# A scan block and two feed-forward layers on one core: one decay transfer per block, and three GpSimd products moved to other engines

## The chip, the cores and the metric

The kernel runs on one core of a Trainium2 chip. The time is the device time of one execution in microseconds (us), and it is given as the median of a few runs. The five engines of the core are called PE (TensorE, matrix products), DVE (VectorE), ACT (ScalarE), POOL (GpSimd) and SP (SyncE, which here only issues transfers). Each works through its own instructions in their order.

## The reference, cut to what matters

```python
# a state-space scan over 4 batches x 8 heads, 768 positions, D = 32, N = 16
log_a = np.log(np.clip(a, 1e-06, 1.0))
for c in range(nc):                              # chunks; state is carried over
    cum = np.cumsum(la, axis=-1)
    L = np.exp(cum[:, :, :, None] - cum[:, :, None, :]) * causal
    M = np.einsum('bhin,bhjn->bhij', Cc, Bc) * L
    y_intra = np.einsum('bhij,bhjd->bhid', M, xc)
    y_inter = np.einsum('bhin,bhnd->bhid', Cc, state) * np.exp(cum)[:, :, :, None]
    y[:, :, sl] = y_intra + y_inter
    Bx = np.einsum('bhjn,bhjd->bhjnd', Bc, xc) * np.exp(cum[:, :, -1:] - cum)[..., None, None]
    state = np.exp(np.sum(la, axis=-1))[:, :, None, None] * state + np.sum(Bx, axis=2)
# then two layers on the 3072 x 256 result, d_ff = 2048
h = x @ w_in;  g = softplus(h);              x = g @ w_out
h = x @ w2_in; g = a smoothed relu of h;     x = g @ w2_out
```

## The kernel before

**Tiling.** The kernel cuts the 768 positions into six blocks `c` of 128 and treats the four batches `b` apart, so that there are 24 units `u = 4c + b` of the scan. A unit holds 8 heads. For each unit the kernel loads x, B and C (`load`, tile `u`) and the rows of the decays (`rows`, tile `ld`), turns the latter into the 128x1024 matrix of decays by a scan on DVE (`decay`, line 745; in block 0 by two products on PE and an Exp on ACT, lines 738 and 747), multiplies the scores C B (`scores`, PE, line 781, one job for two units) by it in two halves (`weigh`, line 790, DVE), and multiplies the result with x on PE (`out`, lines 814 to 826). `evac` (ACT, line 839) and `ready` (DVE, lines 848 and 850) carry the 256 values per position out of PSUM as a high and a low part, `xh` and `xl`.

**Carried state.** From block 1 on three small products join them, all on POOL. `sources` (line 753) weighs B by the last column of the decays, `cd` (line 765) weighs C by the running decays in tile `dec`, and `sm` (line 858) makes two masked copies of the state. `dec` is loaded once per block `c` from a DRAM scratch, by eight transfers, one per head (line 728). In block 0, `sources` is done in two halves, on POOL too.

**Feed-forward steps.** Each layer is 96 or more steps `s`: `up` (PE, lines 881 to 883, three products for each pair of high and low parts), an activation `g` (ACT line 905 in layer one, ACT and DVE in layer two), its split into `g_hi` and `g_lo` (line 920, DVE or POOL), and `down` (PE, line 946). In the first eight steps `down` uses the unsplit weight instead (`whole`, line 934). The weights come in 64-bit form, 16 pieces `j` of 128x512 per layer, into four staging buffers `st` (`load_w`, line 539). Five or six instructions take each piece apart: `w0` and `w1` (ACT or DVE, lines 555, 551, 563, 569), `w2` (DVE, line 575 or 580), `w3` (DVE, line 587), `w_hi` (line 492 or 494) and `split_w` (line 597, DVE or POOL). A staging buffer is free after `w3`.

**Order.** `program()` writes the order of all of it as the kernel is built. It adds each job with its engine or engines, an assumed cost, what it needs, which buffers it takes and returns, and a due time; `Jobs.order` then takes the jobs one by one by a list schedule on assumed times. Where a job has a choice of engines, the constant `BIAS` is added to POOL's time before the two are compared. The constants from `WHOLE` to `WARM` (lines 382 to 412) feed this planner, and so a change in one of them can reorder every engine. What the planner assumes is not what the chip does, and the engines keep the written order whatever happens.

**Fillers.** Before line 1027 the loop puts idle products on PE (line 1022) where the planned gap before a PE job is long, in the first 26 us of the plan only.

Of the kernel before, what the change touches and what calls it, by code (L numbers as in the profile page):

```python
# [7 lines left out]
F32 = mybir.dt.float32  # L8
# [18 lines left out]
class Jobs:  # L27
# [4 lines left out]

    LATENCY = {PE: 200, ACT: 230, DVE: 220, POOL: 200, SP: 1900}

    def __init__(self):
        self.jobs = {}
# [7 lines left out]
    def order(self, slots, begin):  # L46
# [51 lines left out]
        for _ in range(len(jobs)):  # L98
            best = []
            for name in ready:  # L100
                options, _, _, takes, _, _ = jobs[name]
                got = pick(takes, min(at[name].values()))
                if got is None:
                    continue
                starts = {e: max(got[0], at[name][e], clock[e]) for e in options}
                bias = lambda e: BIAS_2 if e == POOL and name[0] == "split_w" and name[1] else BIAS.get(e, 0)
                _, start, engine = min((starts[e] + cost + bias(e), starts[e], e) for e, cost in options.items())
                best.append((start, due[name], number[name], name, engine, got[1]))
            assert best, [(name, jobs[name][3]) for name in ready]
            first = min(best)  # L110
            start, _, _, name, engine, got = min(
                (b for b in best if b[4] == first[4] and b[0] <= first[0] + (PATIENCE if first[0] > EARLY else HASTE)), key=lambda b: (b[1], b[0], b[2])
            )
            options, _, _, _, gives, size = jobs[name]
            for tag, i in got:
                free[tag] = [f for f in free[tag] if f[1] != i]
            held[name] = got
            result.append((name, engine, got))
            cost = options[engine] * (1.9 if engine == PE and start < COLD else 1.0)
            if engine in (DVE, POOL):  # L120

                kind = name if isinstance(name, str) else name[0]
                other = POOL if engine == DVE else DVE
                for a, b, k in busy[other][-3:]:
                    shared = max(0.0, min(b, start + cost) - max(a, start))
                    cost += shared * SHARED[engine].get(kind, 0.0) * (k > 0)
                    if b == clock[other]:
                        clock[other] += shared * k * (SHARED[engine].get(kind, 0.0) > 0)
                busy[engine].append((start, start + cost, SHARED[engine].get(kind, 0.0)))
            clock[engine] = start + cost  # L130
            end = clock[engine]
            if engine == SP:
                pipe = max(pipe, end) + size / RATE
                end = pipe
            done = self.done[name] = end
            end += self.LATENCY[engine]
            self.start[name], self.end[name] = start, end
            if name == ("ready", NU - 1):
                free["z"] += [(end, 0), (end, 1)]
            for other in gives:  # L140
                kept = held[other[1]] if other[0] == "part" else held.pop(other)
                for tag, i in [kept[other[2]]] if other[0] == "part" else kept:
                    free[tag].append((end, i))
            ready.remove(name)
            for other in after[name]:
                for e in at[other]:

                    at[other][e] = max(at[other][e], done + 80 if e == engine != SP else end)
                missing[other] -= 1
                if missing[other] == 0:  # L150
                    ready.add(other)
# [38 lines left out]
def program():  # L190
# [33 lines left out]
    add("clip", DVE, 350, needs=["clip_load", "sums"])  # L224
    add("store", SP, 800, needs=["clip"], size=98e3)
    add("runs", DVE, 1500, needs=["clip", ("columns", 1)])
    add("store_runs", SP, 400, needs=["runs"], size=98e3, gives=["clip_load"])
    for c in range(1, NC):
        add(("dec", c), SP, 400 * DEC_DMAS, needs=["store_runs"], takes=["dec"], size=262e3)
    for u in range(NU):  # L230
# [12 lines left out]
        else:  # L243
            add(("rows", u), SP, 400, needs=["store"], takes=["ld"], size=524e3)
            add(("decay", u), DVE, 2220, needs=[("rows", u)])
            decay = [("decay", u)]
            add(("cd", u), POOL, 400, needs=[("load", u), ("dec", c)])
        if c == 0:
            for hg in range(2):
                add(  # L250
                    ("sources", u, hg), POOL, 400, takes=["bt"] * (hg == 0),
                    needs=[("load", u), ("decay", u, hg)] + ([("sources", u, 0)] if hg else []),
                )
        elif c < NC - 1:
            add(("sources", u), POOL, 450, needs=[("load", u)] + decay, takes=["bt"])
        if b % 2:
            v = u // 2
            add(
# [23 lines left out]
        if c > 1:  # L282
            needs += [("split_w", 0, kind, j) for kind in "io" for j in range(8) if place_of(kind, j) == c]
            needs += [("down", s) for s in range(WHOLE)]
        due = when(first_step[c, b] - LEAD if c < 2 else min(first_step[c, b] - LEAD, CHUNK * (c - 1) + SPACE * b + SHIFT))
        add(("evac", u), ACT, 270 + 150 * (c == 0), needs=needs)
        add(
# [1 line left out]
            gives=[("out", u)] + [("dec", c)] * (b == NB - 1 and c > 0),  # L289
        )  # L290
        if c < NC - 1:
            add(("sm", u), POOL, 330, needs=[("ready", u)])


    last_use, first_use = {}, {}
# [5 lines left out]
    for m in range(2):  # L301
        for j in sorted(range(8), key=lambda j: first_use[m, j]):
            for kind in "io":
                w = (m, kind, j)
                add(("load_w", *w), SP, 400, takes=["st"], size=524e3)
                add(
                    ("w0", *w), {ACT: 580} if signed(*w) else {ACT: 580, DVE: 350}, needs=[("load_w", *w)] + [("ready", NU - 1)] * m, takes=["w32"] * m,
                )
# [13 lines left out]
    for s, (m, c, t0, n, fc, m_fc) in enumerate(steps):  # L322
# [38 lines left out]
        if fc + m_fc == NFC:  # L361
            root = ("down", min(r for r in range(len(steps)) if steps[r][:3] == (m, c, t0)))
            for e in range(2):
# [7 lines left out]
                    )  # L371
                else:
                    add(("store", s, e), SP, 400, due=own, needs=[("finish_hi", s, e)], gives=[("finish_hi", s, e)], size=262e3)
    slots = dict(h=2, y=1, z=0, acc=4, t=2, g=N_G, gh=3, gl=3, ld=5, u=4, bc=3, bt=3, dec=2, st=4, w32=16, osb=4)
    result = jobs.order(slots, {POOL: 3700, ACT: 2000, PE: 4000, DVE: 800})
    return jobs, steps, result


# [2 lines left out]
]  # L381
WHOLE = 8
ACT_UNTIL = 120
H_MORE = 8
H_ALL = 84
GL_POOL = 84
COLD = 0.0
KEEP = 26000.0
FILL = 0.8
SHARED = {  # L390
    DVE: {"w1": 1.1, "w2": 0.95, "w3": 0.95, "decay": 0.36, "split_w": 0.3, "g_lo": 0.1, "clip": 0.3, "runs": 0.3},
    POOL: {"g_lo": 0.25, "weigh": 0.4, "sources": 1.0, "cd": 1.1, "sm": 0.6, "split_w": 0.4},
}
WEIGH_POOL = []
PRELU = (0, 0)
LOW_ACT = 1
BIAS = {DVE: 0, POOL: 500}
PATIENCE = 0
EARLY = 30000.0
HASTE = 0  # L400
CHUNK = 16
BIAS_2 = 2000
RATE = 250.0
BEGIN = 14000.0
STRETCH = 1.0
LEAD = 1
SPACE = 4
SHIFT = 2
LAG = 3000
DEC_DMAS = 8  # L410
N_G = 3
WARM = 10

# [2 lines left out]


@with_exitstack
def tile_kernel(ctx: ExitStack, tc: tile.TileContext, al, bc, ub, w_in, w_out, w2_in, w2_out, out):

# [53 lines left out]
    for tag, dtype, n in (("xh", F32R, NC), ("xl", F32R, NC), ("ld", F32, 5), ("gh", F32R, 3), ("gl", F32R, 3), ("u", F32, 4), ("dec", F32, 2)):  # L476
        for i in range(n):
            new(f"{tag}{i}", dtype, tag) if tag in ("xh", "xl", "gh", "gl") else buf(tag, i)
    raw_t = [base.tile([128, 2, 256, 2], U32, name=f"st{i}") for i in range(4)]
    eye_t = base.tile([128, H * Q], F32, name="eye_t")  # L480
    sm_t = [base.tile([128, 64], F32, name=f"sm{b}") for b in range(NB)]
# [1 line left out]
    idle, eye16, later = (base.tile([128, Q], BF16, name=n) for n in ("idle", "eye16", "later"))  # L483

    xh, xl, xw = {}, {}, {}
    clip_z = dram.tile([NU * 2, 4, Q], F32, name="clip_z")
    clip_p = dram.tile([NU * 2, 4, Q], F32, name="clip_p")
    engines = {ACT: nc.scalar, DVE: nc.vector, POOL: nc.gpsimd}

    def copy(engine, out, in_):  # L490
# [23 lines left out]
    spare += [("ld", 4, 0), ("ld", 4, 1), ("bc", 2, 0), ("w32", 0, 0)] + [("u", i, 0) for i in range(4)]  # L514

    def raw(*w):
        t = raw_t[got["load_w", *w][0][1]]
        return t[:, :, :, 0], t[:, :, :, 1], t

    def w32(m, kind, j):  # L520
# [98 lines left out]
    def a_load(engine):  # L619

        first = new(of("a_load"), F32, "first")
        tiles["a"] = [first[:, i * Q:(i + 1) * Q] for i in range(3)]
        src = al[0:2 * NB].rearrange("r (h i) -> (r h) i", h=4)
        nc.sync.dma_start(tiles["a"][0], src.unsqueeze(0).to_broadcast([4, 32, Q]))
        nc.gpsimd.memset(tiles["a"][2], 1.0)

    @job
# [54 lines left out]
    def store(engine, *step):  # L682
# [3 lines left out]
            for i in range(0, T, n):  # L686
                nc.sync.dma_start(out[steps[s][1], e, :, i:i + n], osb(s, e)[:, i:i + n])
        else:
            nc.sync.dma_start(clip_z, z_t)

    @job
    def runs(engine):
# [5 lines left out]

    @job
    def store_runs(engine):  # L700
        nc.sync.dma_start(clip_p, tiles["clip"])

    @job
    def load_bc(engine, v):
# [12 lines left out]
    @job  # L717
    def rows(engine, u):

        rows_of = clip_z.rearrange("(u g) h i -> u (g h i)", g=2)  # L720
        nc.sync.dma_start(flat(ld_t(u)), rows_of[u:u + 1].to_broadcast([128, H * Q]))

    @job
    def dec(engine, c):
        t = mine("dec", c)[0]
        src = clip_p.rearrange("(c b g) h i -> c (g h) b i", b=NB, g=2)[c]
        for h in range(H):
            nc.sync.dma_start(t[h * N:(h + 1) * N], src[h:h + 1].to_broadcast([N, NB, Q]))

    def ld_t(u):  # L730
        return buf(*got["rows", u][0]) if u >= NB else buf(*got["spread", u, 0][1])
# [18 lines left out]
    def sources(engine, u, hg=None):  # L750

        h = slice(0, H) if hg is None else slice(4 * hg, 4 * hg + 4)
        nc.gpsimd.tensor_tensor(
            out=bt_t(u)[:, h], in0=parts(u)[1].rearrange("p (h n) -> p h n", n=N)[:, h],
            in1=ld_t(u)[:, h, Q - 1:Q].to_broadcast([128, h.stop - h.start, N]), op=ALU.mult,
        )
# [5 lines left out]
    def cd(engine, u):  # L762

        t = parts(u)[2]
        nc.gpsimd.tensor_tensor(out=t, in0=t, in1=mine("dec", u // NB)[0][:, u % NB, :], op=ALU.mult)

    def cb_t(u, hg):
        banks = got["scores", u // 2]
# [86 lines left out]
    @job  # L855
    def sm(engine, u):
        b = u % NB
        nc.gpsimd.tensor_tensor(
            out=sm_t[b].rearrange("p (e d) -> p e d", e=2), in0=s_t[b].rearrange("p (e d) -> p e d", e=2),
            in1=of_one.unsqueeze(2).to_broadcast([128, 2, D]), op=ALU.mult,  # L860
        )


    root = {}
# [208 lines left out]
```

## Time and profile before

| | |
|---|---|
| runs | 607.69, 606.53, 604.54 us; median 606.53 us |
| the profiled execution | 607.7 us, of which the span of instructions is 606.0 us |
| busy share of the span | PE 97%, DVE 78%, ACT 40%, POOL 11% |
| mean granted clock of PE | 0.993 |
| instructions | 9263 |

A row of the profile gives the start of an instruction in us from the span's start, its duration, the engine, the line of the kernel and the tiles as out<-in, and in brackets how long the engine sat idle before it and what ended that. PE's matrix products overlap, so a busy PE is not always a PE at its best rate; the granted clock (1.00 is 2.4 GHz, 0.50 is 1.2 GHz) is listed beside it.

### The profile page before, as it was taken

To read this page: it belongs to the slowest core of one execution; us is meant where nothing else is said; L and a number is where in the kernel's file an instruction comes from. 1 tells how busy PE (TensorE), PEld (TensorE's weight loads), DVE (VectorE), ACT (ScalarE), POOL (GpSimd) and SP (SyncE) were. 2 spreads that over 40 slices of the span, in tenths; PEclk is the share of its full clock that TensorE was granted. 3 is DMA by queue.
4 is the path that set the end of the run, shared out by engine and by line. 5 is a ranking of instruction groups with operands and counts; after the bars stand their busy time and mean duration, and the time that the engine had idled before them with its cause. 6 is when DMAs were issued, how large, how long until landed. Compare 5 with 4: busy or idle time off the path is not lost.

```text
span 606.0 us, 9263 instructions
## 1 busy us (share of the span) xinstructions
PE 587.9 (97%) x3588; PEld 484.7 (80%) x3588; DVE 471.1 (78%) x758; ACT 239.6 (40%) x415; POOL 66.9 (11%) x88
## 2 busy tenths in 40 slices
PE   7897989999999999999999999999999999999997
PEld 3685989998877777777788888888888888888886
DVE  7878999666575765535899986678899898899895
ACT  4544663322222322322576876654232231322321
POOL 4215553310211100000100000000000000000000
PEclk9898999999999999999999999999999999999999
DMA  7975543412322212000344000000000000000000
GB/s 278 322 245 192 180 157 131 131 54 96 104 80 70 79 54 70 1 0 1 105 140 140 35 1 0 2 1 36 35 2 0 36 1 1 36 0 2 35 1 35
DMA packets 22208, 43.69 MB, mean 72 GB/s; under 512 B 2308, under 2 KB 5252, under 8 KB 22164
## 3 DMA queue, kind: packets, MB, share of 16 engines
q1 hardware_dynamic: 22164, 43.10, 21.2%
q8 instruction: 28, 0.46, 0.3%
q14 instruction: 16, 0.13, 0.1%
HBM read 39.75 MB, written 3.34 MB: 71 GB/s over the span
## 4 chain that ended last, share of the span: by engine, by line
PE 88%; DVE 7%; issue 2%; ACT 1%; POOL 1%; DMA 1%; DVEq 0%; POOLq 0%; ACTq 0%
PE acc L946 41%; PE h L881 10%; PE h L882 10%; PE h L883 10%; PE acc L881 2%; PE acc L882 2%; PE acc L883 2%; DVE ld L745 2%; PE acc L934 2%; PE y L819 2%; DVE w L587 2%; PE z L883 1%; PE z L881 1%; PE z L882 1%; PE y L781 1%
## 5 line engine op out<-in xcount | busy, mean ns | idle before, releaser
L946 PE MATMUL acc<-gh,woh 128*128 128x512 f32 (+1 forms) x416 | 149.9, 368 | 0.0
L946 PE MATMUL acc<-gh,wol 128*128 128x512 f32 (+1 forms) x416 | 148.6, 365 | 0.0
L920 DVE TENSOR_TENSOR gl<-g,gh 128x512 fp32r<-128x512 f32 x178 | 125.1, 703 | 13.6 <-ACT gh L492 1.7
L881 PE MATMUL h<-xh,wih 128*128 128x512 f32 (+1 forms) x336 | 122.4, 364 | 1.4 <-ACT g L905 1.4
L882 PE MATMUL h<-xh,wil 128*128 128x512 f32 (+1 forms) x336 | 120.2, 358 | 1.9 <-DVE wil L597 1.9
L883 PE MATMUL h<-xl,wih 128*128 128x512 f32 (+1 forms) x336 | 119.7, 356 | 0.0
L946 PE MATMUL acc<-gl,woh 128*128 128x512 f32 (+1 forms) x416 | 114.1, 365 | 0.0
L494 DVE CAST gh<-g 128x512 fp32r<-128x512 f32 x128 | 54.6, 426 | 61.1 <-ACT g L905 52.8
L946 PEld LDWEIGHTS acc<-gh,woh 128*128 128x128 f32 x416 | 78.4, 188 | 14.6 <-ACT g L905 1.0
L946 PEld LDWEIGHTS acc<-gh,wol 128*128 128x128 f32 x416 | 78.5, 189 | 12.3
L946 PEld LDWEIGHTS acc<-gl,woh 128*128 128x128 f32 x416 | 73.3, 189 | 12.6
L892 ACT ACTIVATE t<-h 128x512 f32<-128x512 f32 x67 | 40.1, 599 | 108.0 <-PE h L883 103.8
L881 PEld LDWEIGHTS h<-xh,wih 128*128 128x128 f32 x336 | 63.5, 189 | 13.5 <-ACT g L905 1.8
L882 PEld LDWEIGHTS h<-xh,wil 128*128 128x128 f32 x336 | 63.6, 189 | 11.2 <-DVE wil L597 2.3
L883 PEld LDWEIGHTS h<-xl,wih 128*128 128x128 f32 x336 | 63.5, 189 | 9.1
L905 ACT ACTIVATE g<-h 128x512 f32<-128x512 f32 x51 | 30.4, 597 | 72.7 <-PE h L883 66.1
L911 DVE SCALAR_TENSOR_TENSOR t<-t 128x512 f32<-128x512 f32 x72 | 49.4, 686 | 6.5 <-ACT t L892 6.1
L745 DVE TENSOR_TENSOR_SCAN ld<-ld,eye_t 128x1024 f32<-128x1024 f32 x20 | 47.1, 2357 | 2.4 <-DMA ld<-clip_z 2.3
L912 DVE TENSOR_TENSOR g<-h,t 128x512 f32<-128x512 f32 x67 | 46.3, 692 | 2.3
L492 ACT CAST gh<-g 128x512 fp32r<-128x512 f32 x56 | 34.8, 621 | 18.7 <-DVE g L912 16.7
L905 ACT ACTIVATE g<-acc 128x512 f32<-128x512 f32 x31 | 18.5, 598 | 48.7 <-PE acc L883 48.1
L881 PE MATMUL acc<-xh,wih 128*128 128x512 f32 (+1 forms) x74 | 26.4, 356 | 0.0
(142 smaller groups left out, 668.4 us busy)
## 6 DMA issues: line engine op xcount, KB each, us to landing
ld<-clip_z SPq DMA_DIRECT2D x20, 512.0 KB, 4.0
st<-in_w_in_dram SPq DMA_DIRECT2D x16, 512.0 KB, 3.8
st<-in_w_out_dram SPq DMA_DIRECT2D x16, 512.0 KB, 4.1
u<-in_ub_dram SPq DMA_DIRECT2D x24, 256.0 KB, 3.8
bc<-in_bc_dram SPq DMA_DIRECT2D x12, 384.0 KB, 3.5
out_dram<-dec SPq DMA_DIRECT2D x6, 256.0 KB, 2.2
dec<-clip_p SPq DMA_DIRECT2D x40, 32.0 KB, 2.8
out_dram<-bc SPq DMA_DIRECT2D x5, 256.0 KB, 2.0
```

The costliest lines, as they stand in the source:

```text
L492: nc.scalar.copy(out, in_)
L494: engines[engine].tensor_copy(out, in_)
L745: nc.vector.tensor_tensor_scan(t, t, eye_t, 0.0, ALU.mult, ALU.add)
L881: nc.tensor.matmul(o, wh, xh[c][:, k, t0:t0 + n], start=(k == 0), stop=False)
L882: nc.tensor.matmul(o, wl, xh[c][:, k, t0:t0 + n], start=False, stop=False)
L883: nc.tensor.matmul(o, wh, xl[c][:, k, t0:t0 + n], start=False, stop=(k == 1))
L892: nc.scalar.activation(out=t, in_=ph, func=AF.Relu, bias=0.5, scale=0.5)
L905: nc.scalar.activation(out=g, in_=ph, func=AF.Softplus)
L911: nc.vector.scalar_tensor_tensor(out=t, in0=t, scalar=1.0, in1=t, op0=ALU.min, op1=ALU.mult)
L912: nc.vector.tensor_tensor(out=g, in0=ph, in1=t, op=ALU.max)
L920: engines[engine].tensor_tensor(out=mine("g_lo", s)[0], in0=mine("g", s)[0], in1=mine("g_hi", s)[0].bitcast(F32), op=ALU.subtract)
L946: nc.tensor.matmul(acc_t(s, e), w, g[:, j * n:(j + 1) * n], start=(begins(e, j) and g is gh and i == 0), stop=(fc + j == NFC - 1 and g is ...
```

## The change

`dec` becomes one transfer for a block instead of eight. For it the DRAM scratch `clip_p` is laid out so that a block's rows lie together, and it is written by four transfers (one for each batch) instead of one; the input `al` is ordered by batch first, and block 0's decays come as an input `a0` of their own. For blocks 1 to 5 `cd` and `sources` run on DVE and `sm` on ACT, there as two instructions; for block 0 `sources` stays on POOL. Two of block 0's `weigh` jobs (numbers 3 and 6, that is unit 1's second half and unit 3's first) go to POOL, each behind a copy of its scores by ACT. The weight pieces `j = 2` of layer one get two staging buffers `sx` in the space of block 1's `xh` and `xl`, so block 1's `evac` needs their `w3`. The planner's constants change with it.

```diff
-    LATENCY = {PE: 200, ACT: 230, DVE: 220, POOL: 200, SP: 1900}
+    LATENCY = {PE: 200, ACT: 230, DVE: 220, POOL: 200, SP: 2300}
...
+            cost += SIGNAL * (engine == DVE)
...
-    add("store_runs", SP, 400, needs=["runs"], size=98e3, gives=["clip_load"])
+    add("store_runs", SP, 1600, needs=["runs"], size=98e3, gives=["clip_load"])
...
-            add(("cd", u), POOL, 400, needs=[("load", u), ("dec", c)])
+            add(("cd", u), DVE, 200, needs=[("load", u), ("dec", c)])
...
-            add(("sources", u), POOL, 450, needs=[("load", u)] + decay, takes=["bt"])
+            add(("sources", u), DVE, 210, needs=[("load", u)] + decay, takes=["bt"])
...
+        if c == 1:
+
+            needs += [("w2" if signed(0, kind, SX) else "w3", 0, kind, SX) for kind in "io"]
...
-            add(("sm", u), POOL, 330, needs=[("ready", u)])
+            add(("sm", u), ACT, 500, needs=[("ready", u)])
...
-                add(("load_w", *w), SP, 400, takes=["st"], size=524e3)
+                add(("load_w", *w), SP, 400, takes=["sx" if m == 0 and j == SX else "st"], size=524e3)
...
-    slots = dict(h=2, y=1, z=0, acc=4, t=2, g=N_G, gh=3, gl=3, ld=5, u=4, bc=3, bt=3, dec=2, st=4, w32=16, osb=4)
-    result = jobs.order(slots, {POOL: 3700, ACT: 2000, PE: 4000, DVE: 800})
+    slots = dict(sx=2, h=2, y=1, z=0, acc=4, t=2, g=N_G, gh=3, gl=3, ld=5, u=4, bc=3, bt=3, dec=2, st=4, w32=16, osb=4)
+    result = jobs.order(slots, {POOL: 3700, ACT: 2000, PE: 5500, DVE: 2500, SP: 900})
...
-H_MORE = 8
+H_MORE = 16
-GL_POOL = 84
+GL_POOL = 16
+SIGNAL = 55.0
-WEIGH_POOL = []
+WEIGH_POOL = [3, 6]
-BIAS = {DVE: 0, POOL: 500}
+BIAS = {DVE: 0, POOL: 2000}
-BIAS_2 = 2000
-RATE = 250.0
+BIAS_2 = 9000
+RATE = 330.0
-SPACE = 4
+SPACE = 2
-LAG = 3000
-DEC_DMAS = 8
+LAG = 1500
+DEC_DMAS = 1
+SX = 2
...
-        src = al[0:2 * NB].rearrange("r (h i) -> (r h) i", h=4)
-        nc.sync.dma_start(tiles["a"][0], src.unsqueeze(0).to_broadcast([4, 32, Q]))
+        nc.sync.dma_start(tiles["a"][0], a0.unsqueeze(0).to_broadcast([4, 32, Q]))
...
-        nc.sync.dma_start(clip_p, tiles["clip"])
+        n = NC * 2
+        for b in range(NB):
+            nc.sync.dma_start(clip_p[:, :, b], tiles["clip"][b * n:(b + 1) * n])
...
-        src = clip_p.rearrange("(c b g) h i -> c (g h) b i", b=NB, g=2)[c]
-        for h in range(H):
-            nc.sync.dma_start(t[h * N:(h + 1) * N], src[h:h + 1].to_broadcast([N, NB, Q]))
+        src = clip_p.rearrange("(c g) h b i -> c (g h) (b i)", g=2)[c]
+        nc.sync.dma_start(flat(t), src.unsqueeze(1).to_broadcast([H, N, NB * Q]))
...
-        nc.gpsimd.tensor_tensor(
+        engines[engine].tensor_tensor(
             out=bt_t(u)[:, h], in0=parts(u)[1].rearrange("p (h n) -> p h n", n=N)[:, h],
...
-        nc.gpsimd.tensor_tensor(out=t, in0=t, in1=mine("dec", u // NB)[0][:, u % NB, :], op=ALU.mult)
+        nc.vector.tensor_tensor(out=t, in0=t, in1=mine("dec", u // NB)[0][:, u % NB, :], op=ALU.mult)
...
-        nc.gpsimd.tensor_tensor(
-            out=sm_t[b].rearrange("p (e d) -> p e d", e=2), in0=s_t[b].rearrange("p (e d) -> p e d", e=2),
-            in1=of_one.unsqueeze(2).to_broadcast([128, 2, D]), op=ALU.mult,
-        )
+        for e in range(2):
+            nc.scalar.activation(
+                out=sm_t[b][:, e * D:(e + 1) * D], in_=s_t[b][:, e * D:(e + 1) * D], func=AF.Copy, scale=of_one[:, e:e + 1],
+            )
```

## Rows read from the trace of the kernel before

**Rows 1.** Windows of the first 100 us: length, then each engine's busy us; at the end PE clock, DMA share, GB/s.
```profile
23.10:27.00 3.90, 3.88 (x33) 2.74 (x33) 3.47 (x7) 0.52 (x1) 0.00 (x0) 0.64 1.03 311
...
38.00:44.00 6.00, 5.09 (x43) 4.70 (x45) 6.00 (x5) 2.62 (x5) 1.11 (x2) 1.00 0.72 210
...
47.00:52.40 5.40, 5.31 (x16) 4.13 (x16) 5.40 (x8) 1.89 (x3) 2.41 (x4) 0.68 0.36 135
...
sum 100.00, PE 85.45 PEld 71.15 DVE 87.52 ACT 50.21 POOL 42.81; mean PE 4.07 PEld 3.39 DVE 4.17 ACT 2.39 POOL 2.04
```

**Rows 2.** Windows of the span: one of layer two.
```profile
320.00:340.00 20.00, 20.00 (x90) 16.57 (x89) 19.81 (x38) 12.74 (x22) 0.00 (x0) 1.00 0.38 127
```

**Rows 3.** Windows from 120 to 245 us, their sum.
```profile
sum 125.00, PE 125.00 PEld 102.39 DVE 79.41 ACT 35.53 POOL 16.73; mean PE 20.83 PEld 17.07 DVE 13.23 ACT 5.92 POOL 2.79
```

**Rows 4.** Timeline of PE to 150 us.
```profile
23.12 2.70 PE L934 MATMUL acc<-gh,w 128*128 128x256 f32 x8 [2.04 <-DVE w L587]
...
30.24 3.62 PE L934 MATMUL acc<-gh,w 128*128 128x256 f32 x16
...
40.92 0.39 PE L882 MATMUL h<-xh,wil 128*128 128x256 f32 x1 [0.91 <-DVE wil L597]
...
47.09 5.41 PE L934 MATMUL acc<-gh,w 128*128 128x256 f32 x16 [2.08 <-DVE w L587]
```

**Rows 5.** The chain that ended last, from 17 us: start, us, what.
```profile
17.25 0.76 POOL bt L753
18.01 0.26 POOL sm L858
18.27 2.46 DVE ld L790 x4
```

**Rows 6.** Groups by line and shape: busy us, mean ns | idle before, releaser.
```profile
L765 POOL TENSOR_TENSOR u<-u,dec 128x128 f32<-128x128 f32 x20 | 17.6, 886 | 20.6 <-DMA u<-in_ub_dram 20.6
L790 DVE TENSOR_TENSOR ld<-acc,ld 128x512 f32<-128x512 f32 x25 | 16.7, 680 | 0.0
...
L587 DVE SCALAR_TENSOR_TENSOR w<-st,w 128x512 uint32<-128x512 uint32 x17 | 15.0, 888 | 0.2
...
L575 DVE SCALAR_TENSOR_TENSOR w<-w,t 128x512 uint32<-128x512 uint32 x15 | 12.9, 864 | 5.0 <-ACT t L563 4.7 <-ACT w L555 0.3
...
L920 POOL TENSOR_TENSOR gl<-g,gh 128x512 fp32r<-128x512 f32 x6 | 11.5, 1921 | 61.0 <-PE acc L946 56.9 <-ACT gh L492 3.4 <-DVE gh L494 0.7
...
L597 POOL TENSOR_TENSOR wol<-w,woh 128x512 fp32r<-128x512 f32 x4 | 8.8, 2206 | 6.1 <-ACT woh L492 5.5 <-PE y L826 0.6
...
L850 DVE SCALAR_TENSOR_TENSOR s<-s,dec,y 128x64 f32<-128x64 f32 x16 | 4.3, 271 | 0.0
...
L841 ACT COPY s<-y 128x64 f32<-128x64 f32 x4 | 0.9, 218 | 0.0
```

**Rows 7.** Timeline of SP from 24 us; xN merges neighbouring issues.
```profile
24.54 10.19 SPq L728 DMA_DIRECT2D dec<-clip_p  x8
34.84 0.40 SPq L539 DMA_DIRECT2D st<-in_w_out_dram  x1
```

**Rows 8.** Waits of SP's queue over the span: us, times, longest.
```profile
SPq L539 <- DVE w L587: 33.0, 11, 7.3
...
SPq L728 <- DMA ld<-clip_z: 6.4, 6, 2.0
```

**Rows 9.** Timeline of all engines around 57 us.
```profile
55.98 2.65 POOL L597 TENSOR_TENSOR wol<-w,woh 128x512 fp32r<-128x512 f32 x1 [0.58 <-PE y L826]
...
57.47 1.71 DVE L575 SCALAR_TENSOR_TENSOR w<-w,t 128x512 uint32<-128x512 uint32 x1
...
60.44 0.68 DVE L575 SCALAR_TENSOR_TENSOR w<-w,t 128x512 uint32<-128x512 uint32 x1
```

**Rows 10.** Timeline of DVE from 47 us.
```profile
46.96 0.68 DVE L790 TENSOR_TENSOR ld<-y,ld 128x512 f32<-128x512 f32 x1
47.56 0.68 DVE L790 TENSOR_TENSOR ld<-acc,ld 128x512 f32<-128x512 f32 x1
```

More of the change, by code (lines that the diff above doesn't have):

```diff
@@ L418, in tile_kernel @@
 @with_exitstack
-def tile_kernel(ctx: ExitStack, tc: tile.TileContext, al, bc, ub, w_in, w_out, w2_in, w2_out, out):
+def tile_kernel(ctx: ExitStack, tc: tile.TileContext, a0, al, bc, ub, w_in, w_out, w2_in, w2_out, out):
     nc = tc.nc
@@ L478, in tile_kernel @@
             new(f"{tag}{i}", dtype, tag) if tag in ("xh", "xl", "gh", "gl") else buf(tag, i)
+    raw_x = {}
     raw_t = [base.tile([128, 2, 256, 2], U32, name=f"st{i}") for i in range(4)]
@@ L485, in tile_kernel @@
     xh, xl, xw = {}, {}, {}
-    clip_z = dram.tile([NU * 2, 4, Q], F32, name="clip_z")
-    clip_p = dram.tile([NU * 2, 4, Q], F32, name="clip_p")
+    clip_z = dram.tile([NU, H * Q], F32, name="clip_z")
+    clip_p = dram.tile([NC * 2, 4, NB, Q], F32, name="clip_p")
     engines = {ACT: nc.scalar, DVE: nc.vector, POOL: nc.gpsimd}
@@ L516, in raw @@
     def raw(*w):
-        t = raw_t[got["load_w", *w][0][1]]
+        tag, i = got["load_w", *w][0]
+        if tag == "sx" and i not in raw_x:
+            raw_x[i] = new(("xh1", "xl1")[i], U32, "raw").rearrange("p a (k f w) -> p (a k) f w", k=1, w=2)
+        t = raw_t[i] if tag == "st" else raw_x[i]
         return t[:, :, :, 0], t[:, :, :, 1], t
@@ L688, in store @@
         else:
-            nc.sync.dma_start(clip_z, z_t)
+            nc.sync.dma_start(clip_z.rearrange("u (g h i) -> (u g) h i", g=2, i=Q), z_t)
     @job
@@ L718, in rows @@
     def rows(engine, u):
-        rows_of = clip_z.rearrange("(u g) h i -> u (g h i)", g=2)
-        nc.sync.dma_start(flat(ld_t(u)), rows_of[u:u + 1].to_broadcast([128, H * Q]))
+        c, b = divmod(u, NB)
+        r = b * NC + c
+        nc.sync.dma_start(flat(ld_t(u)), clip_z[r:r + 1].to_broadcast([128, H * Q]))
     @job
@@ L1042 @@
     c6 = C.reshape(NB, H, NC, Q, N)
-    al = np.ascontiguousarray(a6.transpose(2, 0, 1, 3)).reshape(NC * NB * 2, 4 * Q)
+    al = np.ascontiguousarray(a6.transpose(0, 2, 1, 3)).reshape(NB * NC * 2, 4 * Q)
+    a0 = np.ascontiguousarray(a6[:, :, 0]).reshape(NB * H, Q)
     by_g = lambda v: v.reshape(NB // 2, 2, 2, 2, 2, NC, Q, N).transpose(5, 0, 1, 2, 4, 7, 3, 6)
@@ L1058 @@
     given = {
-        "al": al, "bc": bc, "ub": ub,
+        "a0": a0, "al": al, "bc": bc, "ub": ub,
         "w_in": bits(moe_w_in), "w_out": bits(moe_w_out), "w2_in": bits(moe2_w_in), "w2_out": bits(moe2_w_out),
```

## The prediction

> **What bounds the kernel now.** I read the windows first, because the page's shares are averages over stages with different limits. In layer two PE is busy for all of a 20 us window at full clock although DVE is busy for 19.81 of it [rows 2], and from 120 to 245 us PE is busy for all 125 us [rows 3]. In these stages PE sets the time, and a change that leaves its products alone gains nothing. What can be gained lies in the first 100 us: there PE is busy for 85.45, so 14.55 us are empty, and DVE is busy for 87.52 [rows 1]. The timeline of PE then shows where the gaps are and who ends them: 2.04 us at 23.12, 0.91 at 40.92 and 2.08 at 47.09, each ended by DVE with a piece of a weight (lines 587 and 597) [rows 4]. After the two long gaps the granted clock is 0.64 and 0.68 of full speed over the windows that follow, so it spent part of them at 1.2 GHz; around the gap of 0.91 us it stayed at 1.00 [rows 1]. The price of that can be read off: sixteen products of line 934 take 3.62 us at full clock and 5.41 behind the gap, 1.79 more [rows 4]. So the question is whether DVE delivers those pieces sooner. Last I read the chain of waits before the first gap: it runs through POOL's `sources` and `sm` into four `weigh` on DVE [rows 5].
>
> **First gap (23.12 us).** Two of block 0's eight `weigh` leave DVE. Back to back, one costs 0.60 us of DVE (46.96 to 47.56) [rows 10], so 2 x 0.60 = 1.20 are saved. `sm` also leaves the POOL stretch of the chain, where it held 0.26 [rows 5]. On the other side POOL gets two products of 128x512; the nearest row is `g_lo` on POOL, 1.92 us [rows 6], against 0.60 on DVE, and ACT gets two copies and the `sm` pairs. If a POOL product lands ahead of `sources` on the chain, up to 1.92 are lost. Bounds: -1.46 to +1.92. I take **-1.2**, since only two of eight move and the later ones of unit 3 are not what PE waits for at 23.12. For the half-speed clock behind this gap, eight products took 2.70 where half of 3.62 is 1.81 [rows 4]: 0.9 on them alone. The gap shrinks to 2.04 - 1.2 = 0.84, and one of 0.91 left the clock at 1.00; but other matter lies close by, so of the 0.9 I take **-0.6**, bounds -1.8 (the full price at 47.09) and 0.
>
> **`dec` in one transfer.** Before, eight issues stretched over 10.19 us and the load of a `w_out` piece stood behind them at 34.84 [rows 7]. Of this stretch 6.4 us at most (over the span) were waits for `ld` transfers in flight [rows 8]; they may stay. Then the load goes out at the earliest at about 25 and at the latest at 24.54 + 6.4 + 0.4 = 31.3, so 3.5 to 9.8 us sooner. What it feeds is the `w3` that PE gets at 47.09. Two more staging buffers act in the same direction: SP's queue waited 33.0 us in 11 waits for `w3` to free a buffer [rows 8]. The four writes of `clip_p` add three issues of some 0.4, before anything waits on them. In price the two gaps at 40.92 and 47.09 are 0.91 + 2.08 = 2.99. Against it DVE gets, before 47 us, about three `sources` and three `cd`. No row has this operation on DVE: below it lies the 128x64 at 0.271, above it the 128x512 at 0.680 [rows 6]; by size it is nearer the lower, and 0.08 of each overlaps the next (0.68 long, 0.60 apart [rows 10]), so I take 0.25, six of them 1.5. Result **-1.5**, bounds -2.99 (cover by idle DVE) and 0 (the planner puts the piece behind the scans as before). With the gap near 1 us the clock should stay up as it did at 40.92: **-1.8** for the sixteen products, bounds -1.8 and 0.
>
> **55 to 100 us.** DVE's `w2` and `w3` took 864 and 888 ns in the mean [rows 6] and 0.68 us when alone [rows 9]: 15 x 0.18 + 17 x 0.21 = 6.3 us lost, most of it in this stage. One place shows how: POOL's `split_w` ran from 55.98 to 58.63, and the `w2` that began at 57.47 ended at 59.18, 0.55 after it [rows 9]. The higher `BIAS` and lower `GL_POOL` take such work from POOL. But its six `g_lo` and four `split_w` [rows 6] would then cost 0.60 each on DVE, 6.0 if all return; and some ten `cd` and `sources` of this stage at 0.25 add 2.5. Net 6.0 + 2.5 - 6.3 = +2.2 if DVE has no idle time to take them; -3.8 if the 6.0 fit into idle time. These ends stand about as far on either side of nothing, and I take **0**.
>
> The Trainium skill's page "SBUF — State Buffer", section "Who interferes with whom", says that a DVE instruction with two SBUF inputs and a GpSimd instruction exclude each other: the later one waits for the whole of the earlier. The trace agrees (1.71 us in place of 0.68 in rows 9). By that rule the two new POOL products speak against the change, and the first term would be +2.6 instead of -1.2; this is rival B.
>
> **After 100 us.** Of 20 `cd` [rows 6] and 16 `sources` (four blocks of four units) some 16 are counted above; the other 20 at 0.25 are 5 us of DVE. They are hidden by DVE's idle time, 125.0 - 79.4 = 45.6 us from 120 to 245 [rows 3]; without that cover they would cost these 5 us. `sm` on ACT is two instructions near 0.218 [rows 6], 8.7 us for all twenty, beside an ACT that is busy for 35.5 of those 125 [rows 3]. POOL keeps nearly nothing. I take **0**, bounds 0 and the price of rival D.
>
> **The sum.** -1.2 - 0.6 - 1.5 - 1.8 + 0 + 0 = -5.1 us. The profiled execution took 607.7 (606.0 span, 1.7 around it), 1.2 above the median of the three runs: 602.6 from the one, 601.4 from the other. The runs lie on both sides of the median, so I go a third of the way from it, from a base of 606.9, and predict **601.8**.
>
> **Rivals.**
> A is the forecast, 601.8, for itself 597.5 to 604.
> B: POOL's two long products block DVE in the first 20 us. Each could hold a `w2`, `w3` or `split_w` for 1.92 [rows 6]: 3.84 - 1.20 = +2.6, and the clock term goes. That is 3.8 + 0.6 worse than A: 606.2. For it speaks the `w2` of 1.71 [rows 9]; against it that `weigh` itself, with one input in PSUM, keeps near 680 ns in the mean [rows 6], and that DVE does mostly this in the stretch.
> C: DVE is the bound of the first 100 us and the gaps only move. Its work there falls by 1.2 and 6.3 and rises by 6.0 + 1.5 + 2.5 = 10.0, so by 2.5 in all, and the clock drops remain: between 606.9 (idle time takes it) and 609.4, say 608. For it speaks that DVE is busy for 87.52 of 100 [rows 1]; against it that the named gaps come from single late pieces.
> D, the slow one: `cd` waits for its unit's `u` load at the head of DVE's queue. On POOL those waits were 20.6 us in the idle column [rows 6], where nobody stood behind them. On DVE `g_hi`, `g_lo` and the next `weigh` stand behind, and `down` on PE waits for these. If more than 8 of the 20.6 reach PE, the gain of 5.1 is gone and 3 us with it (the bound of "slower"); at three quarters it is +15.4 - 5.1: 617; at half, 612. Against it: the planner places `cd` by when it expects the load, and DVE has 45.6 us to spare [rows 3].
> E: every term comes out at its lower bound: -1.46 - 1.8 - 2.99 - 1.8 - 3.8 = -11.8, so 595.
>
> **How the numbers follow.** A 0.54, B 0.09, C 0.16, D 0.12, E 0.09. About 3 us (0.5%) is what a measurement here can tell from no change, so the bounds are 603.5 and 609.6. A but for its upper tail (0.50) and E give faster 0.59; that tail (0.04), B and two thirds of C (0.11) give 0.24; D and the rest of C 0.17. The range reaches from E to past B and C: 595.5 to 608.5, leaving D and a little of E out.
>
> **What would show it.** Right: in the profile after, PE's busy time in the first 100 us rises from 85.45 to 89 or more; no gap of 2 us before line 934; clock 1.00 in the windows that had 0.64 and 0.68; `w2` and `w3` under 0.75 us in the mean; the third and fourth `w_out` loads issued by 31 us. Wrong: long idle times of DVE before line 774 ended by a DMA (D); `w2` of 1.5 us or more before 23 us beside POOL's line 792 (B); gaps of the same sum at other lines (C). It is wrong altogether if PE is no longer busy throughout from 120 us on, as everything above takes this part as fixed.

## The result, and the profile after

The changed kernel takes 599.83 us (median of six runs, 598.23 to 601.92), the kernel before 607.09 (six runs beside it). The ratio is 0.9883, with a 95% interval of 0.9857 to 0.9909: faster by 7.1 us by the ratio, where the forecast was 5.1 us and the range 595.5 to 608.5. The profiled execution took 598.3 us, its span 596.6.

Windows of the kernel after, columns as in [rows 1]:

```profile
20.00:30.00 10.00, 7.19 (x87) 6.12 (x86) 9.60 (x15) 8.78 (x21) 3.42 (x3) 1.00 0.96 325
30.00:40.00 10.00, 9.98 (x59) 8.95 (x59) 10.00 (x12) 5.22 (x9) 1.60 (x1) 1.00 1.05 317
40.00:50.00 10.00, 10.00 (x70) 9.48 (x69) 10.00 (x15) 5.29 (x10) 5.84 (x1) 1.00 0.53 194
50.00:60.00 10.00, 9.94 (x78) 9.55 (x77) 10.00 (x17) 8.79 (x16) 2.61 (x2) 1.00 0.71 211
60.00:80.00 20.00, 19.85 (x221) 17.95 (x219) 18.28 (x32) 9.63 (x22) 3.50 (x2) 1.00 0.58 175
80.00:100.00 20.00, 20.00 (x240) 18.27 (x237) 16.15 (x28) 7.26 (x16) 0.00 (x0) 1.00 0.40 135
sum 100.00, PE 94.08 PEld 78.68 DVE 90.60 ACT 57.70 POOL 28.00; mean PE 11.76 PEld 9.84 DVE 11.32 ACT 7.21 POOL 3.50
```

The kernel before, in the same windows:

```profile
20.00:30.00 10.00, 7.96 (x82) 6.44 (x80) 7.93 (x16) 3.97 (x9) 0.67 (x2) 0.83 0.86 288
30.00:40.00 10.00, 10.00 (x65) 9.17 (x63) 6.15 (x8) 3.72 (x7) 0.00 (x0) 1.00 0.74 252
40.00:50.00 10.00, 7.01 (x49) 5.99 (x49) 9.96 (x12) 3.69 (x6) 6.49 (x7) 0.90 0.71 226
50.00:60.00 10.00, 8.35 (x88) 6.27 (x87) 8.48 (x9) 4.32 (x8) 4.63 (x4) 0.92 0.53 170
60.00:80.00 20.00, 18.97 (x183) 17.97 (x184) 19.91 (x26) 12.89 (x23) 10.69 (x8) 1.00 0.52 173
80.00:100.00 20.00, 18.03 (x170) 17.23 (x169) 19.00 (x26) 10.41 (x20) 11.41 (x10) 1.00 0.50 167
```

In the first 100 us PE is busy for 94.08 in place of 85.45 [rows 1], and the clock stays at 1.00 in this execution. From 40 to 60 us it is busy for 19.94 in place of 15.36, so 4.58 us of gaps are gone there, and from 60 to 100 us another 2.85. From 120 to 245 us nothing changed: PE is busy throughout, as in [rows 3].

```profile
sum 125.00, PE 125.00 PEld 101.25 DVE 78.87 ACT 42.48 POOL 0.00; mean PE 125.00 PEld 101.25 DVE 78.87 ACT 42.48 POOL 0.00
```

PE's timeline after (line 946 is the old 934, line 793 the old 781):

```profile
23.37 1.99 PE L946 MATMUL acc<-gh,w 128*128 128x256 f32 x8 [1.60 <-ACT gh L917]
...
29.13 0.39 PE L895 MATMUL h<-xl,wih 128*128 128x256 f32 x1 [1.21 <-DVE xl L860]
...
30.42 3.62 PE L946 MATMUL acc<-gh,w 128*128 128x256 f32 x16
...
43.35 3.62 PE L946 MATMUL acc<-gh,w 128*128 128x256 f32 x16
...
61.88 0.48 PE L793 MATMUL y<-bc 32*128 32x256 f32 x2
```

and rows of PE and of DVE before:

```profile
43.87 0.48 PE L781 MATMUL y<-bc 32*128 32x256 f32 x2
```
```profile
31.72 0.69 DVE L575 SCALAR_TENSOR_TENSOR w<-w,t 128x512 uint32<-128x512 uint32 x1 [2.72 <-ACT t L563]
...
36.66 0.69 DVE L575 SCALAR_TENSOR_TENSOR w<-w,t 128x512 uint32<-128x512 uint32 x1 [2.00 <-ACT t L563]
...
38.00 2.28 DVE L745 TENSOR_TENSOR_SCAN ld<-ld,eye_t 128x1024 f32<-128x1024 f32 x1
...
40.78 4.68 DVE L745 TENSOR_TENSOR_SCAN ld<-ld,eye_t 128x1024 f32<-128x1024 f32 x2
```

Three things are to be seen. The first sixteen products of line 946 start at 30.42, before at 30.24 [rows 4]: up to there nothing was gained. The scores of block 1, at 43.87 before, come at 61.88: PE works on feed-forward steps at 43 us. And DVE, the engine that ended PE's gaps, is busy for 19.6 of the 20 us from 20 to 40 in place of 14.1. Before, it stood idle for 4.7 us behind two of ACT's pieces, and three decay scans of block 1 came after that, ahead of the piece that PE waited for at 47.09 [rows 4]; after, the first scan starts at 31.14. So the orders of PE and of DVE both differ.

### The profile page after: what moved, and what is told of

Its sections match the earlier page's. It is cut to its first block, busy times and chain, and to the rows that moved or that the text cites. A ratio compares the mean times of both kernels' runs of the same rounds, so it can differ in the third digit from the quotient of the medians.

```text
span 596.6 us, 9199 instructions
## 1 busy us (share of the span) xinstructions
PE 587.1 (98%) x3596; PEld 483.8 (81%) x3596; DVE 472.4 (79%) x787; ACT 255.1 (43%) x465; POOL 28.0 (5%) x31
## 4 chain that ended last, share of the span: by engine, by line
PE 89%; DVE 7%; issue 2%; ACT 1%; DMA 1%; DVEq 0%
PE acc L958 42%; PE h L893 10%; PE h L894 10%; PE h L895 10%; PE acc L893 2%; PE acc L894 2%; PE acc L895 2%; PE y L831 2%; PE z L894 2%; PE z L895 2%; PE z L893 2%; PE y L793 2%; DVE w L598 1%; PE y L826 1%; DVE w L586 1%
## 5 line engine op out<-in xcount | busy, mean ns | idle before, releaser
L893 PE MATMUL h<-xh,wih 128*128 128x512 f32 (+1 forms) x330 | 119.7, 363 | 0.0
L895 PE MATMUL h<-xl,wih 128*128 128x512 f32 (+1 forms) x330 | 117.5, 356 | 1.2 <-DVE xl L860 1.2
L894 PE MATMUL h<-xh,wil 128*128 128x512 f32 (+1 forms) x330 | 117.6, 356 | 0.2
L502 DVE CAST gh<-g 128x512 fp32r<-128x512 f32 x124 | 52.9, 426 | 56.2 <-ACT g L917 47.9
L904 ACT ACTIVATE t<-h 128x512 f32<-128x512 f32 x63 | 37.8, 600 | 112.0 <-PE h L895 109.9
L894 PEld LDWEIGHTS h<-xh,wil 128*128 128x128 f32 x330 | 62.3, 189 | 9.3 <-DVE wil L608 0.6
L924 DVE TENSOR_TENSOR g<-h,t 128x512 f32<-128x512 f32 x63 | 43.6, 691 | 2.2
L500 ACT CAST gh<-g 128x512 fp32r<-128x512 f32 x60 | 37.2, 620 | 18.2 <-DVE g L924 16.8
L917 ACT ACTIVATE g<-acc 128x512 f32<-128x512 f32 x28 | 16.8, 599 | 38.3 <-PE acc L895 38.2
L893 PE MATMUL acc<-xh,wih 128*128 128x512 f32 (+1 forms) x68 | 24.1, 355 | 0.0
```

The source lines that it names most:

```text
L500: nc.scalar.copy(out, in_)
L502: engines[engine].tensor_copy(out, in_)
L893: nc.tensor.matmul(o, wh, xh[c][:, k, t0:t0 + n], start=(k == 0), stop=False)
L894: nc.tensor.matmul(o, wl, xh[c][:, k, t0:t0 + n], start=False, stop=False)
L895: nc.tensor.matmul(o, wh, xl[c][:, k, t0:t0 + n], start=False, stop=(k == 1))
L904: nc.scalar.activation(out=t, in_=ph, func=AF.Relu, bias=0.5, scale=0.5)
```

## The experiments

Ratios are to the kernel before, on the same chip. Theory P is the prediction's (less work on GpSimd, one decay transfer and two more buffers let VectorE deliver sooner), theory O that the new order makes the gain.

### e1 and e2: the planner's assumed transfer rate

```diff
-RATE = 250.0
+RATE = 330.0
```
in the kernel before (e1), and the reverse in the kernel after (e2).

> The kernel before with one constant of its planner changed: the assumed transfer rate is 330 in place of 250. No instruction changes its engine, its size or its number; only the order can change. In the plan the scan of block 1 moves behind more feed-forward steps (its second unit pair's first product from 47 to 65 us of plan time). Theory O (the gain is the order: PE gets feed-forward work in place of block 1's scan while the weights' pieces come): 598 to 602 us, ratio 0.985 to 0.993. Theory P (the prediction's: fewer GpSimd products, one decay transfer and two staging buffers let VectorE deliver sooner): nothing of that is in here, so 606 to 608, ratio 0.998 to 1.003.

> The changed kernel with the assumed transfer rate back at 250; all its moved products, the single decay transfer and the two staging buffers stay. Theory O: most of the gain is given back, 604 to 608 us, ratio 0.995 to 1.003. Theory P: 599 to 602, ratio 0.987 to 0.992.

e1: 601.28 us, 0.9902 [0.9878, 0.9927]. e2: 604.68 us, 0.9968 [0.9953, 0.9983]. One constant gives 0.98% of the 1.17%, and without it the whole of the other edits gives 0.32%. Windows of e1, and its `g_lo` on GpSimd:

```profile
40.00:50.00 10.00, 8.57 (x62) 7.50 (x61) 9.93 (x7) 6.09 (x10) 6.53 (x4) 1.00 0.82 272
50.00:60.00 10.00, 9.18 (x71) 8.59 (x71) 9.86 (x19) 7.44 (x14) 2.46 (x1) 1.00 0.69 218
```
```profile
L920 POOL TENSOR_TENSOR gl<-g,gh 128x512 fp32r<-128x512 f32 x9 | 19.4, 2157 | 79.1 <-PE acc L946 62.3 <-ACT gh L492 12.0 <-DVE gh L494 4.7
```

PE is busy for 17.75 of these 20 us. The expectation is wrong in one point: the planner chose other engines too for some jobs that have a choice. GpSimd got nine `g_lo` in place of six [rows 6] and is busy for 80.0 us in place of 66.9, so less work on GpSimd isn't where e1's gain comes from. The scores of block 1 stand at 46.50 here, nearly as early as before, so their late place in the changed kernel isn't needed for the gain. What e1 shares with it is that VectorE starts on the scans early:

```profile
28.10 5.50 DVE L745 TENSOR_TENSOR_SCAN ld<-ld,eye_t 128x1024 f32<-128x1024 f32 x2
```

From 20 to 40 us VectorE is busy for 19.9 us in e1. Over all the profiles it is busy there for 19.1 to 20.0 us in the changed kernel and in e1, e3, e4, e5, e6, e9, e11 and e12, and for 12.7 to 15.6 in the kernel before and in e2, e7, e8 and e10; the first nine are the ones with a ratio under 0.993. No run moves the scans alone, so this goes with the gain and isn't shown to make it by itself.

In e2 the planner writes a third order, with gaps of its own; its PE timeline:

```profile
20.85 4.42 PE L1034 MATMUL h<-idle 128*128 128x512 bf16 x10 [2.97 <-DVE ld L802]
...
63.81 0.46 PE L826 MATMUL y<-u,sm 32*64 32x128 f32 x8 [2.07 <-DVE u L777]
```

The second gap is ended by `cd`, now on VectorE: in that order it stands too late, behind other work. So e2 doesn't tell the rate's part from that of an unlucky order alone. In e1 `cd`, `sources`, `sm` and the transfers stay as they were before, and the gain is there.

### e3, e4, e6, e9: the edits undone in the new order

The order of the changed kernel is kept as the planner wrote it, and only the engine or the transfer is put back:

```diff
     result = jobs.order(slots, ...)
+    result = [(n, POOL if n[0] in ("cd", "sources", "sm") else e, got) for n, e, got in result]   # e3
+    result = [(n, DVE if n[0] == "weigh" else e, got) for n, e, got in result]                    # e6
```
For e4, `dec` and `store_runs` stand as in the kernel before; e9 is all of these together. e6 leaves out ScalarE's copies, and VectorE reads the scores from a PSUM bank that a later product may have overwritten by then: its data are not the reference's then, and only its time is read. In e9 it reads the copies. Besides the order and the two buffers, all four keep the planner's choice of engine for the jobs that have one, `g_lo` and `split_w` among them.

> The changed kernel with its order written down as it is, and cd, sources of blocks 1 to 4 and sm put back on GpSimd at their places in that order. Theory O: within 1.5 us of the changed kernel, 599 to 601.5. Theory P: the exclusion of GpSimd and VectorE costs VectorE some 0.2 to 1 us at each of about ten products before 100 us while 36 x 0.25 us leave it: 602 to 605 us.

> The changed kernel in its own order, with the decay transfers as before: eight for a block, from a scratch written by one transfer with rows of 512 bytes. Theory P (the prediction's second term): the weights' loads behind the first two go out 3.5 to 9.8 us later and the term of 1.5 to 3.3 us comes back: 601.5 to 603. Theory O: block 1's scan comes late enough for it, and other loads go out by at most some us later with nothing waiting: 599 to 601.

> The changed kernel in its own order, with the two weigh products of block 0 done on VectorE at their places and without ScalarE's copies for them. Theory P (first term): 2 x 0.60 us come back to VectorE before the first step's product with the unsplit weight, +1 to +2 us: 601 to 603. Rival B (the long GpSimd products hold VectorE): VectorE gets their time back, 597 to 599. Theory O: the first 25 us are bound by several engines at once and the gain lies behind 40 us, so within 1 us of the changed kernel.

> The changed kernel in its own order with the moves undone together: cd, sources and sm on GpSimd, eight decay transfers for a block, and the two weigh products of block 0 on VectorE (from the copies that ScalarE still makes). What stays of the change is the order and the two staging buffers. Theory O: 599 to 602.5 us, ratio 0.987 to 0.993. Theory P: the terms of the prediction come back, 604 to 607.

For comparison the changed kernel was run again (e5).

> The changed kernel itself, as the measure on this chip for the kernels of the same call: 598 to 602 us by either theory, ratio 0.986 to 0.991.

| kernel | median us | ratio | interval |
|---|---|---|---|
| e5, the changed kernel | 600.28 | 0.9886 | 0.9857 to 0.9915 |
| e3, products on GpSimd | 602.16 | 0.9891 | 0.9847 to 0.9936 |
| e4, eight decay transfers | 601.69 | 0.9894 | 0.9856 to 0.9931 |
| e6, weigh on VectorE | 600.13 | 0.9883 | 0.9849 to 0.9917 |
| e9, all of these undone | 601.82 | 0.9901 | 0.9866 to 0.9935 |

Every interval holds 0.9886. With all the moves undone, a gain of 1.0% stays of the 1.17%. Not all went as theory O said: the medians of e3 and e4 lie above its ranges and inside those of theory P, and by their medians e3, e4 and e9 are 1.4 to 1.9 us behind e5. The lowest times of e3 and e4 (598.08 each) are as low as that of the changed kernel (598.23). Four or five executions of each don't settle whether the moved products have a part in these 1.4 to 1.9 us; what they look like in the profiles shows below (e12).

### e7 and e10: the edits done in the old order

e7 moves `cd`, `sources` and `sm` in the order of the kernel before, with one line as above; e10 puts the single decay transfer into it.

> The kernel before in its own order, with cd and the sources of blocks 1 to 4 on VectorE and sm on ScalarE at their places in that order. Theory P: VectorE loses some 0.25 us for each and gets back what GpSimd's products cost it, so 605 to 606.5. Theory O: nothing of the order changes, so PE still waits for the same late pieces: 606 to 608, ratio 0.998 to 1.003. Rival D (cd waits at the head of VectorE's queue for its load): 609 or more.

> The kernel before in its own order, with the decay rows brought by one transfer for a block (and the scratch, its four writes and the inputs laid out for it); nothing else moves. The prediction's second term: the third and fourth pieces of w_out go out 3.5 to 9.8 us sooner, the gaps at 40.9 and 47.1 us shrink, 603 to 605.5 us. Theory O: VectorE's order still puts the piece behind three decay scans, so the load lands sooner and waits there: 606 to 608.

e7: 607.73 us, 0.9997 [0.9985, 1.001]. e10: 607.61 us, 1.0009 [0.9992, 1.0027]. Neither gives anything. e10 tests the prediction's second term; its timelines of SP's queue, of VectorE and of PE:

```profile
24.55 0.84 SPq L729 DMA_DIRECT2D dec<-clip_p  x1
26.31 0.37 SPq L539 DMA_DIRECT2D st<-in_w_out_dram  x1
```
```profile
39.22 4.68 DVE L746 TENSOR_TENSOR_SCAN ld<-ld,eye_t 128x1024 f32<-128x1024 f32 x2
43.83 0.83 DVE L575 SCALAR_TENSOR_TENSOR w<-w,t 128x512 uint32<-128x512 uint32 x1
```
```profile
23.12 1.97 PE L935 MATMUL acc<-gh,w 128*128 128x256 f32 x8 [2.04 <-DVE w L587]
...
45.53 5.41 PE L935 MATMUL acc<-gh,w 128*128 128x256 f32 x16 [2.09 <-DVE w L587]
```

The load goes out at 26.31 in place of 34.84 [rows 7], 8.5 us sooner and inside the bounds given. Its `w2` still runs at 43.83, behind the scans, and PE's gap is 2.09 us as before. Here a piece that lands sooner is worth nothing, as the written order makes it wait.

### e8: what the half-speed clock costs

```diff
+            for s, near in ((0, 1), (4, 5)):
+                if name == ("down", s):
+                    ...                  # nine idle products into the bank of up step `near`
             emit[kind](engine, *args)
```

> The kernel before, with nine idle products of 0.21 us put on PE ahead of each of the two down products that wait for VectorE at 23 and 47 us; they work in the gap and change nothing else. If the half-speed clock behind the gaps costs what the rows say (0.9 to 1.8 us each) and is brought on by the gaps, the time falls to 603 to 605 and the granted clock is 1.00 throughout; if it hides behind another wait, the time stays at 606 to 607.5.

604.58 us, 0.9957 [0.9945, 0.997]. Windows of e8:

```profile
20.00:30.00 10.00, 10.00 (x99) 7.66 (x98) 7.84 (x16) 5.13 (x11) 0.83 (x2) 1.00 0.87 276
...
85.00:90.00 5.00, 5.00 (x33) 5.00 (x33) 5.00 (x8) 2.22 (x4) 2.08 (x1) 0.72 0.53 159
```

The two gaps are as long as before but filled with idle work, and the clock holds; the gain is 0.0043 x 607.1 = 2.6 us. Not all of the expectation held: in the profiled execution (606.04 us) the clock falls once, later, behind gaps of 0.71 and 1.01 us at 82 and 83 us.

### e11: no extra staging buffers

```diff
-... takes=["sx" if m == 0 and j == SX else "st"], size=524e3)
+... takes=["st"], size=524e3)
```
with the wait of block 1's `evac` for them removed.

> The changed kernel without the two extra staging buffers; the planner writes a new order, in which the scores of block 1 come before the eighth step and its first output product still at 68 us of plan time. Theory O: the pieces j = 2 come later, but PE's order still keeps block 1's products behind the feed-forward steps, 600 to 602.5 us. Theory P: the term of the staging buffers comes back, 602 to 604.

599.17 us, 0.9873 [0.9851, 0.9896]: not slower than e5 at 0.9886, and a little under theory O's range. The planner puts the scores of block 1 at 41.58 us here and its output products late, and PE is busy for 95.34 of the first 100 us. The two buffers aren't needed for the gain.

### e12: idle products in the gaps that are left

Seven idle products go ahead of the first `down` of the changed kernel, five ahead of the third `up`, in the manner of e8.

> The changed kernel with seven idle products on PE ahead of the first down product (where PE waits 1.6 us for ScalarE) and five ahead of the third up step (1.2 us for VectorE). If its slower runs (600.4 to 602.8) are those in which the clock falls once behind these gaps, the median falls to 598 to 599.5 and the spread to under 2 us; if not, it stays at 600 or rises by up to 1 us for the idle products.

601.89 us, 0.9926 [0.9908, 0.9943]: outside both expectations, and 0.4% above e5, whose interval it just overlaps. The two gaps are filled, but another opens. The timelines of PE and of GpSimd in e12, and one of its windows:

```profile
62.17 1.13 PE L958 MATMUL acc<-gl,woh 128*128 128x256 f32 x4 [2.65 <-POOL gl L932]
```
```profile
54.67 8.68 POOL L932 TENSOR_TENSOR gl<-g,gh 128x512 fp32r<-128x512 f32 x2 [8.92 <-ACT gh L500]
```
```profile
60.00:65.00 5.00, 2.83 (x13) 2.83 (x14) 1.43 (x3) 2.85 (x5) 3.35 (x2) 0.73 0.72 208
```

The same two products of GpSimd, and VectorE beside them, in the changed kernel's first profile:

```profile
55.19 1.70 POOL L932 TENSOR_TENSOR gl<-g,gh 128x512 fp32r<-128x512 f32 x1 [9.22 <-DVE w L562]
59.09 1.65 POOL L932 TENSOR_TENSOR gl<-g,gh 128x512 fp32r<-128x512 f32 x1 [2.20 <-ACT gh L500]
```
```profile
55.67 1.78 DVE L608 TENSOR_TENSOR wil<-w,wih 128x512 fp32r<-128x512 f32 x1
```

There VectorE lost 1.1 us on one instruction beside GpSimd's first product, and GpSimd finished at 56.89. In e12 GpSimd's first product began some tenths of a microsecond sooner, VectorE's instructions followed each other without a gap, and the two `g_lo` on GpSimd took 8.68 us together; PE waited 2.65 for them and then ran at a mean clock of 0.73. The profiles of e3, e4 and e9 show the same (9.10, 8.57 and 8.62 us on GpSimd; 3.12, 2.54 and 3.11 of PE's time), those of e5, e6 and the first one of the changed kernel don't (two products of 1.6 to 1.7). The four executions with it took 601.2 to 602.8 us, the three without it 598.3 to 599.3. So what happens at 55 us is worth some 3 us. What decides it isn't shown: the only difference seen is some tenths of a microsecond in when the instructions meet. That this also makes the spread of the changed kernel's own runs, 598.2 to 602.8, is likely and was not shown, as only two of them were profiled.

## Why the prediction was right, and where its steps were not

**The bound was read rightly.** PE sets the time after 100 us, and nothing changed there; the gain is made before, and it is PE's gaps and the clock. The two profiled executions are 9.4 us apart (607.7 and 598.3). Up to 30 us the changed kernel is 0.18 behind. From 40 to 60 us PE has 4.58 us fewer of gaps, from 60 to 100 us 2.85, and the sixteen products that took 5.41 at half speed take 3.62, which is 1.79. That makes 9.0 of the 9.4. The 7.1 by the ratio are less, as other executions of the changed kernel took longer.

**The clock terms** (0.6 + 1.8 = 2.4 us) were right in size for the kernel before: 2.6 by e8, with both gaps filled. In the changed kernel only the second brought time: the eight products behind the first gap took 1.99 in place of 2.70, and at 30 us nothing of that was left. The first of them isn't certain in a single execution: behind the same gap of 2.04 us, the eight products took 1.97 in e10's profile, where the clock stayed at 1.00; before they took 2.70 and the clock fell to 0.64 [rows 1].

**The first gap** (-1.2) failed. The gap is 1.60 in place of 2.04, but the product behind it starts at 23.37 in place of 23.12. VectorE did save its two `weigh`, and ACT became late: its copies and `sm` pairs were named in this term and put at nothing without a reason. ACT's timeline after, and of before:

```profile
17.06 0.52 ACT L871 ACTIVATE sm<-s,of_one 128x32 f32<-128x32 f32 x2
...
20.87 0.54 ACT L871 ACTIVATE sm<-s,of_one 128x32 f32<-128x32 f32 x2
21.43 1.28 ACT L916 ACT_TABLE_LOAD   x1
22.72 0.60 ACT L917 ACTIVATE gh<-h 128x512 f32<-128x512 f32 x1
```
```profile
19.24 1.28 ACT L904 ACT_TABLE_LOAD   x1
20.53 0.60 ACT L905 ACTIVATE gh<-h 128x512 f32<-128x512 f32 x1
```

The first softplus comes 2.2 us later, behind two pairs of `sm`, a copy of scores and the weight pieces that the new buffers let in. ACT was busy almost throughout that stretch before the change too, and I summed it over 125 us of another stage. Rival B did not decide either: GpSimd's two products took 1.34 and 1.75 us, one `w2` lost 0.5 to the first, and e6 without them stays at 0.9883.

**The decay transfer** (-1.5) failed as a mechanism by itself. The load came 8.5 us sooner, as worked out, and the gap stayed (e10). "The planner puts the piece behind the scans as before" stood as the bound of nothing, and in the old order it is what happens. The gaps at 40.9 and 47.1 did go, with the new order: e1 shows 84% of the gain (0.98 of 1.17%) with the assumed rate alone. The 4.58 us gained there are also more than this term's far bound of 2.99, as that counted two gaps and not the smaller ones up to 60 us. The fourth `w_out` load goes out at 23.74 in the changed kernel, so this sign came true while its reason didn't hold.

**55 to 100 us** (0). This term was too small: 2.85 us of PE's gaps are gone from 60 to 100 us, and no run says by which edit. That GpSimd's work would mostly return to VectorE did not hold:

```profile
L598 DVE SCALAR_TENSOR_TENSOR w<-st,w 128x512 uint32<-128x512 uint32 x15 | 11.3, 756 | 0.0
L608 POOL TENSOR_TENSOR wol<-w,woh 128x512 fp32r<-128x512 f32 x4 | 10.8, 2705 | 15.1 <-ACT woh L500 15.1
L586 DVE SCALAR_TENSOR_TENSOR w<-w,t 128x512 uint32<-128x512 uint32 x10 | 7.8, 780 | 0.0
...
L932 POOL TENSOR_TENSOR gl<-g,gh 128x512 fp32r<-128x512 f32 x3 | 6.1, 2036 | 20.0 <-ACT gh L500 10.8 <-DVE w L562 9.2
...
L586 DVE SCALAR_TENSOR_TENSOR w<-w,g 128x512 uint32<-128x512 uint32 x6 | 5.7, 950 | 0.0
...
L777 DVE TENSOR_TENSOR u<-u,dec 128x128 f32<-128x128 f32 x20 | 5.5, 281 | 0.0
```

Four `split_w` and three `g_lo` stay on GpSimd, and `w2` and `w3` still take 756 to 950 ns in the mean, not under 750. `cd` has no idle time before it, so rival D's wait for the load did not come in this order (in e2's PE did wait 2.07 us for a `cd`); its price of 281 ns is near the 0.25 us taken. Rivals C and E are out with the result.

So the place was right, the clock and the gaps from 40 us on, and the reason was not, and that the sum came near is in part luck. The first gap and its clock were to bring 1.8 us and brought nothing. The terms for 40 to 100 us were to bring 3.3 and brought 9.2 in the profiled execution (4.58 + 1.79 + 2.85). And the 3.3 rested on a load that in the old order brings nothing when it comes sooner. What closes the gaps is the planner's new order, with its choices of engine: VectorE's instructions became little shorter (`w3` 756 ns in place of 888), but it works from 20 to 40 us, where it stood idle for 5.9. The prediction named the planner's constants and priced only what they moved between engines.

## What to carry to other kernels

Where a planner writes the order, read a change of its constants as the change: run the old kernel with the new constant alone before giving the moved instructions any credit, and look which jobs it put on another engine as well. An earlier landing or a shorter instruction is worth something only if what follows it in its engine's written order moves up as well. And in the stage that is to gain, sum every engine that gets work, not only those that lose it.

## What the runs showed of the hardware that was not expected

A GpSimd product with an unbroken row of VectorE instructions beside it can last several times as long: two took 8.68 us together (e12; 9.10, 8.57 and 8.62 in e3, e4 and e9) where they took 1.6 to 1.7 each in other executions of the same order. The Trainium skill's page "SBUF — State Buffer", section "Who interferes with whom", says that the later of the two waits for the earlier one. One such wait is what the 1.78 us in place of 0.68 of VectorE's looks like; with one wait for each of GpSimd's products an estimate is 2 x (1.7 + 0.68) = 4.8 us and not 8.68. That GpSimd waits for several VectorE instructions in turn is a reading that no run here tests.

Idle products held the clock over gaps of 2 us (e8, 2.6 us won). In e12 the kernel took longer with the same means: GpSimd's products at 55 us began some tenths of a microsecond sooner and came out long. Whether the idle products caused that wasn't tested apart.
